# Recalibrating the build-time scheduler of a fused attention, expert and two-layer kernel: a floor on start times, measured durations, weight lows on VectorE, paced conversion

## The chip, the cores and the metric

The kernel runs on one core of one Trainium2 chip. The metric is the device time of one execution in microseconds (us); lower is better. The engines are TensorE (PE in the profile, with its weight loads as PEld), VectorE (DVE), ScalarE (ACT), GpSimd (POOL) and SyncE (SP), which here only issues DMAs. Each engine runs its own instructions in the order in which the program lists them, and waits on semaphores for the others.

## The reference

```python
attn = softmax(scale * q @ k.T, causal window of 64)      # 4 batches, 8 heads, 576 tokens, width 64
x    = (attn @ v).reshape(2304, 512)
e    = argmax(x @ w_gate + modality_bias[modality_id])    # one of 8 experts per token
x    = gate_w * (relu(x @ w1[e]) @ w2[e])                 # 512 -> 1024 -> 512
h    = x @ w_in                                           # 512 -> 2048
out  = (h - tanh(h)) @ w_out                              # 2048 -> 512
```

`w_in` and `w_out` come as float64, everything else as float32.

## The kernel before, in words

Full float32 precision is made of two reduced-precision parts: each operand is split into a high part and a low part (operand minus its high part), and each product is three matmuls, high by high, low by high, high by low. So every weight tile needs a **high copy** (`wh`, a cast) and a **low** (`wl`, a subtraction).

There are two stages. The **second stage** (`second`, the two-layer part) is a loop written out by hand; it starts on TensorE when the first stage's last matmul is done. The **first stage** (`front`) holds everything else:

- Attention runs in 36 groups (9 for each batch): scores (line 560), softmax on ScalarE, VectorE and GpSimd, transposes (line 584), values (line 605).
- Routing runs once for each batch (`route`): logits, softmax gate, expert ids, and a table of token positions. The gated rows go to memory as `xs`. After the last batch `unit_table` makes a table of the remaining work in some 55 tiny VectorE instructions (lines 818 to 966).
- The experts run as 5 units of tokens (units 0 to 3 have 504 tokens, unit 4 has 288). Units 0 and 1 can start while attention still runs. A unit gathers its rows with 4 GpSimd DMAs (`xg`, line 1033), transposes them on TensorE (line 1051) and splits them (`xh`, `xl`). Its **layer 1** is 96 matmuls (line 1125) with hidden parts `hh` on ScalarE (line 1156) and `hl` on VectorE (line 1159) in 8 pieces; its **layer 2** is 96 matmuls (line 1145) in 4 pieces. The 16 weight tiles of a unit are loaded to `raw`, and split by `t_wsplit` to `wh` and `wl`, in rings of 4 buffers each. `t_ids` turns a unit's token ids with one small TensorE transpose (line 1186) of `pif`, which VectorE copies (line 1183).
- The conversion (`t_conv`, 32 tiles) makes float32 bits out of the float64 words of `w_in` and `w_out`: two ScalarE instructions, three VectorE ones (lines 1220, 1222, 1224, here called the conversion's three steps) and a GpSimd addition (lines 1228 or 1235); 12 of the tiles are then split too (`winH`, `winL`, line 1241).

What sets the order of the first stage is a list scheduler that runs when the program is built. Each piece of work is a generator (a thread) that yields an `Op`: engine choices with a planned duration, tokens that it waits for, buffer rings, a PSUM bank, a priority. `Flow.pick` takes the op that can start first by the plan, lets ops with several engine choices go to the one that ends first (with `BIAS` added for VectorE), and writes the instruction; that fixes each engine's order. The chip does not follow the plan's times, only its order. An op with no engine (`Op(None, deps)`) is a group of conditions:

```python
            if not op.eng:
                return None, t, th
```

In the kernel before, the time at which such a group held is forgotten: the thread's next op, if it names no token itself, may be planned earlier than that time.

Of the kernel before, what the change touches and what calls it, by code (L numbers as in the profile page):

```python
# [109 lines left out]
class Flow:  # L110

    LAG = dict(PE=0.3, DVE=0.08, ACT=0.08, POOL=0.1, SP=0.0)
    BIAS = dict(DVE=0.3)
    LOOK = 0.05

    def __init__(self):
        self.free = dict(PE=6.0, DVE=5.0, ACT=5.0, POOL=8.0, SP=3.0)
        self.wire, self.th, self.n = 0.0, [], 0
        self.bank = [Tok(0.0) for _ in range(8)]

    def add(self, gen, prio):
        self.n += 1
        th = [prio, self.n, gen, None]
        self.th.append(th)
        self.step(th, None)

    def step(self, th, r):
        try:
            th[3] = th[2].send(r)
        except StopIteration:  # L130
            self.th.remove(th)

    def ready(self, op):
        t = 0.0
# [16 lines left out]
    def pick(self):  # L151
        best = {}
        for th in self.th:
            op = th[3]
            t = self.ready(op)
            if t is None:
                continue
            if not op.eng:
                return None, t, th
            e = min(op.eng, key=lambda e: max(self.free[e], t) + op.eng[e] + (len(op.eng) > 1) * self.BIAS.get(e, 0.0))  # L160
            best.setdefault(e, []).append((max(self.free[e], t), th))
        assert best, "nothing can go on"
        e = min(best, key=lambda e: min(s for s, _ in best[e]))
        lo = min(s for s, _ in best[e]) + self.LOOK
        prio = lambda th: (th[0] if th[3].prio is None else th[3].prio, th[1])
        s, th = min((x for x in best[e] if x[0] <= lo), key=lambda x: prio(x[1]))
        return e, s, th

    def run(self):
        while self.th:  # L170
            e, s, th = self.pick()
            op, r = th[3], Done()
            r.e, r.s, r.rel = e, s, [g.take() for g in op.rings]
            r.t = s
# [12 lines left out]


class Kernel:
# [179 lines left out]
    def t_load(self):  # L369
        nc, ap, at, R = self.nc, self.ap, self.at, self.rings  # L370

        def qk(pi):
            r = yield Op(("SP", DQ if pi == 0 else 2 * DQ), rings=[R["qk"]], prio=2.25 * pi - 4, wire=2.1)
            if pi:
                self.load_qk(pi)
            self.raw["qkr", pi] = r.rel[0]
            self.tk("qk", pi).t = r.t

        def tail(b):
            r = yield Op(("SP", 2 * DQ), rings=[R["tl"]], prio=9 * b, wire=1.1)  # L380
            tl = at.tile([128, 8, 64], F32, name="tl")
            nc.sync.dma_start(tl[64:128], ap["k"][b, :, 512:576, :].rearrange("h p d -> p h d"))
            nc.sync.dma_start(tl[0:64], ap["q"][b, :, 512:576, :].rearrange("h p d -> p h d"))
            self.raw["t", b] = tl, r.rel[0]
            self.tk("tl", b).t = r.t

        def v(pi):
            b, hp = divmod(pi, 4)
            h0 = 2 * hp
            r = yield Op(("SP", 2 * DQ), rings=[R["va"]], prio=2.25 * pi - 2, wire=1.1)  # L390
            va = at.tile([128, 4, 2, 64], F32, name="va", bufs=3)
            vb = at.tile([128, 3, 2, 64], F32, name="vb", bufs=3)
# [4 lines left out]
            r = yield Op(("SP", 2 * DQ), [r.tok], prio=2.25 * pi - 1, wire=0.5)
# [240 lines left out]
    def t_xrow(self, t):  # L638
# [13 lines left out]
        else:  # L652
            nc.vector.tensor_scalar(xr, pf, g, None, op0=ALU.mult)
        bk.t = r.t
        r = yield Op(("SP", DQ), [r.tok], wire=0.9)
        nc.sync.dma_start(self.xs[t * 128 : t * 128 + 128, :], xr)
        rel.t = r.t
        self.tk("xs", t).t = r.t
# [311 lines left out]
    def t_flag(self, okB, tok):  # L970
# [1 line left out]
        r = yield Op(("POOL", 1.4), [tok])  # L972
        self.Ti = self.cp.tile([BR, E * NSLOT], I32, name="Ti")
        nc.gpsimd.tensor_copy(self.Ti, self.T)
        r = yield Op(("PE", 0.1), [tok], bank=self.bankX)
        ps, bk = self.bt(r, 128, 1), r.bt
        nc.tensor.matmul(ps, self.ones[0:1, :], okB, start=True, stop=True)
        r = yield Op(("DVE", 0.6), [r.tok])
# [44 lines left out]
    def t_gather(self, i):  # L1023
# [2 lines left out]
        u = self.us[i]  # L1026
        yield Op(None, self.tks("xs", range(u.rows)))
        for j, _, _ in u.blocks:
            r = yield Op(("POOL", 1.12), [], [R["xg"]] if j == 0 else [], wire=0.9, lag=6.0)
            if j == 0:  # L1030
                u.xgr = r.rel[0]
                u.xg = mo.tile([BR, CB, DM], F32, name="xg")
# [57 lines left out]

    def t_wsplit(self, i, s, w, tok, rel):
        nc, mo, R = self.nc, self.mo, self.rings
        r = yield Op(dict(ACT=0.62, DVE=0.45), [tok], [R["wh"]])
        hi, rh = mo.tile([128, DM], F32R, name="wh", bufs=NW), r.rel[0]
        self.copy(r, hi, w)
        self.ws[i, s, 0] = hi, rh
        self.tk("ws", i, s, 0).t = r.t
        r = yield Op(dict(DVE=0.69, POOL=1.4), [r.tok], [R["wl"]])
        lo, rl = mo.tile([128, DM], F32R, name="wl", bufs=NW), r.rel[0]
        self.eng(r).tensor_tensor(lo, w, hi.bitcast(F32), op=ALU.subtract)  # L1100
        rel.t = r.t
# [74 lines left out]
    def t_ids(self, i):  # L1176
# [4 lines left out]
        rel = r.rel[0]  # L1181
        f = self.cp.tile([BR, CB], F32, name="pif")
        nc.vector.tensor_copy(f[:, :n], u.ids[:, :n])
        r = yield Op(("PE", 0.2), [r.tok], bank=self.bankX)
        ps, bk = self.bt(r, n, BR), r.bt
        nc.tensor.transpose(ps, f[:, :n], self.idF[:BR, :BR])
        r = yield Op(("DVE", 0.2), [r.tok])
# [12 lines left out]

    def t_conv(self, n, t):
        nc, cv, R = self.nc, self.cv, self.rings
        yield Op(None, [self.tk("w", *t), self.tk("O", CONV0)])
        r = yield Op(("SP", DQ), [], [R["craw"]], wire=1.8)
        raw, rr = self.conv_load(*t), r.rel[0]
        hi = raw.rearrange("p (n two) -> p n two", two=2)[:, :, 1]
        hf = raw.bitcast(F32).rearrange("p (n two) -> p n two", two=2)[:, :, 1]
# [520 lines left out]
```

## Time and profile before

| | |
|---|---|
| median of 3 runs | 812.12 us (810.32 to 814.28) |
| the profiled execution's own time | 808.94 us |
| its span, first to last instruction | 807.2 us |
| TensorE busy | 751.1 us (93%) |
| VectorE busy | 654.5 us (81%) |
| ScalarE busy | 504.3 us (62%) |
| GpSimd busy | 338.1 us (42%) |

The span is what the trace covers; the profiled execution's time is 1.7 us more. Busy shares are means over two stages that are limited differently: in the second stage TensorE is never idle for long, so the shares say little about the first. Times within the trace count from its first instruction.

### The profile page before, as it was taken

How to read it: one execution, taken by the hardware profiler on the slowest of the kernel's cores; microseconds unless marked ns; L12 is line 12 of the kernel's file. 1: busy time of each engine (PE TensorE's matmuls, PEld its weight loads, DVE VectorE, ACT ScalarE, POOL GpSimd, SP SyncE). 2: the span in 40 equal slices, each digit the busy share in tenths (PEclk: the TensorE clock that was granted, in tenths of full speed). 3: DMA queues.
4: the chain of work that ended last, by engine and by line, in shares of the span. 5: the costliest groups of instructions: out<-in, count | busy, mean ns of one | idle time of the engine just before them, and what ended most of it. 6: DMA issues, size and time to landing. Idle time of an engine off the chain costs nothing.

```text
span 807.2 us, 13452 instructions
## 1 busy us (share of the span) xinstructions
PE 751.1 (93%) x4489; PEld 655.1 (81%) x4495; DVE 654.5 (81%) x1140; ACT 504.3 (62%) x1195; POOL 338.1 (42%) x324
## 2 busy tenths in 40 slices
PE   6999859898969879999899999999999999999994
PEld 5888748677848667789888999988999989999893
DVE  4777829779999999827599888888888888888873
ACT  4788728663544454312789777777776767777662
POOL 3424235525656575220669344333324424434222
PEclk9999969999979989999999999999999999999997
DMA  9878767464768775535101011010101101001001
GB/s 192 161 184 191 195 139 213 130 220 148 232 213 255 234 206 169 160 117 159 36 1 40 0 40 30 11 40 10 31 1 40 40 0 40 22 1 39 1 2 43
DMA packets 131733, 80.39 MB, mean 100 GB/s; under 512 B 67988, under 2 KB 124820, under 8 KB 131654
## 3 DMA queue, kind: packets, MB, share of 16 engines
q1 hardware_dynamic: 127350, 69.55, 31.9%
q0 software_dynamic: 3264, 9.63, 3.9%
q8 instruction: 37, 0.61, 0.3%
q14 instruction: 42, 0.34, 0.2%
q10 hardware_dynamic: 1040, 0.26, 0.1%
HBM read 62.10 MB, written 14.16 MB: 94 GB/s over the span
## 4 chain that ended last, share of the span: by engine, by line
PE 75%; DVE 13%; issue 5%; POOL 2%; ACT 2%; DMA 2%; DVEq 0%; POOLq 0%; ACTq 0%
PE ps_g L1528 24%; PE ps_q L1574 24%; PE bank L1145 7%; PE bank L1125 6%; PE bank L560 4%; PE bank L605 2%; PE bank L584 2%; DVE hl L1159 1%; DVE wh L303 1%; DVE cva L1220 1%; POOL xg L1033 1%; DVE cva L1224 1%; DVE wl L1100 1%; DMA xg<-xs,ids 1%; PE bank L450 1%
## 5 line engine op out<-in xcount | busy, mean ns | idle before, releaser
L1559 POOL TENSOR_TENSOR gl<-gv,gh 128x384 fp32r<-128x384 f32 x94 | 100.5, 1070 | 167.5 <-ACT gh L1558 167.2
L1550 DVE COPY_PREDICATED gv<-gm,gt 128x384 f32<-128x384 int32 x96 | 110.8, 1154 | 9.9
L1574 PE MATMUL ps_q<-H,gh 128*128 128x512 f32 x288 | 113.5, 394 | 0.0
L1574 PE MATMUL ps_q<-H,gl 128*128 128x512 f32 x288 | 113.1, 395 | 0.2 <-DVE gl L1559 0.2
L1558 ACT ACTIVATE gh<-gv 128x384 fp32r<-128x384 f32 x96 | 50.3, 524 | 90.9 <-issue 77.4
L1546 DVE SCALAR_TENSOR_TENSOR gv<-gu,ps_g 128x384 f32<-128x384 f32 x96 | 52.9, 551 | 42.9 <-ACT gt L1543 42.3
L1548 DVE SCALAR_TENSOR_TENSOR gv<-gs,gv 128x384 f32<-128x384 f32 x96 | 77.3, 805 | 3.3
L1100 POOL TENSOR_TENSOR wl<-raw,wh 128x512 fp32r<-128x512 f32 x30 | 44.0, 1467 | 57.3 <-DVE wh L303 21.3
L1574 PEld LDWEIGHTS ps_q<-H,gl 128*128 128x128 f32 x288 | 54.0, 188 | 13.3 <-DVE gl L1559 0.7
L1547 DVE SCALAR_TENSOR_TENSOR gv<-gs,gv 128x384 f32<-128x384 f32 x96 | 60.1, 626 | 3.3
L580 POOL TENSOR_TENSOR P<-P,rc 128x512 f32<-128x512 f32 x36 | 38.0, 1058 | 58.8 <-DVE rc L578 26.9
L1542 ACT ACTIVATE gs<-gu,pa 128x384 f32<-128x384 f32 x96 | 58.0, 604 | 5.7 <-DVE gv L1548 5.7
L1541 ACT ACTIVATE gs<-gu,pa 128x384 f32<-128x384 f32 x96 | 59.3, 618 | 3.4 <-DVE gv L1547 0.2
L1574 PEld LDWEIGHTS ps_q<-H,gh 128*128 128x128 f32 x288 | 54.1, 188 | 8.9
L1545 ACT ACTIVATE gm<-gu,pth 128x384 f32<-128x384 f32 x96 | 58.0, 604 | 0.0
L574 ACT ACTIVATE P<-bank,nm 128x128 f32<-128x128 f32 x144 | 50.8, 373 | 7.7 <-DVE nm L571 7.5
L1549 DVE TENSOR_TENSOR gt<-ps_g,gt 128x384 f32<-128x384 f32 x96 | 52.7, 549 | 0.0
L303 DVE CAST wh<-raw 128x512 fp32r<-128x512 f32 x60 | 35.2, 591 | 19.1 <-PE bank L1145 17.2
L1100 DVE TENSOR_TENSOR wl<-raw,wh 128x512 fp32r<-128x512 f32 x50 | 43.9, 885 | 3.6 <-PE bank L1125 1.9
L1540 ACT ACTIVATE gu<-ps_g 128x384 f32<-128x384 f32 x96 | 45.4, 473 | 0.0
L1145 PE MATMUL bank<-hh,wh 128*128 128x504 f32 (+1 forms) x160 | 40.0, 385 | 5.5 <-ACT hh L1156 3.4
L1543 ACT ACTIVATE gt<-ps_g 128x384 f32<-128x384 f32 x96 | 45.0, 469 | 0.0
(420 smaller groups left out, 2105.3 us busy)
## 6 DMA issues: line engine op xcount, KB each, us to landing
raw<-in_w SPq DMA_DIRECT2D x80, 256.0 KB, 3.2
craw<-in_wout SPq DMA_DIRECT2D x16, 512.0 KB, 4.8
craw<-in_win SPq DMA_DIRECT2D x16, 512.0 KB, 4.7
xs<-xr SPq DMA_DIRECT2D x18, 256.0 KB, 2.2
kr<-in_k SPq DMA_DIRECT2D x16, 256.0 KB, 4.0
va<-in_v SPq DMA_DIRECT2D x32, 128.0 KB, 3.4
yd<-ys SPq DMA_DIRECT2D x16, 252.0 KB, 3.5
qr<-in_q SPq DMA_DIRECT2D x15, 256.0 KB, 4.3
```

Source lines behind the costliest of these rows:

```text
L1100: self.eng(r).tensor_tensor(lo, w, hi.bitcast(F32), op=ALU.subtract)
L1145: nc.tensor.matmul(ps, wt[:, k % 4, :], h, start=(q == 0), stop=(q == 3 * NF1 - 1))
L1528: nc.tensor.matmul(ps, w[:, c, :], x[:, c, :], start=(c == 0 and i == 0), stop=(c == 3 and i == 2))
L1541: nc.scalar.activation(s1, u, AF.Square, bias=self.pa1)
L1542: nc.scalar.activation(s2, u, AF.Square, bias=self.pa2)
L1545: nc.scalar.activation(m, u, AF.Relu, bias=self.pth)
L1546: nc.vector.scalar_tensor_tensor(v, u, cA, ps, op0=ALU.mult, op1=ALU.mult)
L1547: nc.vector.scalar_tensor_tensor(v, s1, b1, v, op0=ALU.add, op1=ALU.mult)
L1548: nc.vector.scalar_tensor_tensor(v, s2, b2, v, op0=ALU.add, op1=ALU.mult)
L1550: nc.vector.copy_predicated(v, m.bitcast(I32), t)
L1559: (nc.vector if last else nc.gpsimd).tensor_tensor(gl, v, gh.bitcast(F32), op=ALU.subtract)
L1574: nc.tensor.matmul(self.po[t], g[:, t * 128 : t * 128 + 128], w, start=(f == 0 and i == 0), stop=(f == NF2 - 1 and i == 2),)
```

## The change

It keeps, for each thread, the time at which a group of conditions held (`th[4]`, the floor) and plans no later op of that thread, or of a thread that it starts, before it. It replaces planned durations and DMA lags, raises the bias against VectorE for ops with a choice, lets weight lows (`wl`, `winL`) go to VectorE alone, has the conversion of tile n wait in the plan until 118 + 6.3 n, and plans the two small transposes of `t_ids` and `t_flag` 8 us after their inputs.

```diff
+CONVT, CONVP = 118.0, 6.3
+SLACK = 8.0
...
-    BIAS = dict(DVE=0.3)
+    BIAS = dict(DVE=0.6)
...
-        th = [prio, self.n, gen, None]
+        th = [prio, self.n, gen, None, self.floor]
...
     def step(self, th, r):
+        old, self.floor = self.floor, th[4]
         try:
             th[3] = th[2].send(r)
         except StopIteration:
             self.th.remove(th)
+        self.floor = old
...
             if t is None:
                 continue
+            t = max(t, th[4])
...
+            else:
+                th[4] = s
...
-        r = yield Op(("PE", 0.2), [r.tok], bank=self.bankX)
+        r = yield Op(("PE", 0.2), [Tok(r.t + SLACK)], bank=self.bankX)
...
-            r = yield Op(("POOL", 1.12), [], [R["xg"]] if j == 0 else [], wire=0.9, lag=6.0)
+            r = yield Op(("POOL", 1.12), [], [R["xg"]] if j == 0 else [], wire=0.9, lag=8.0)
...
-        r = yield Op(dict(ACT=0.62, DVE=0.45), [tok], [R["wh"]])
+        r = yield Op(dict(ACT=0.63, DVE=0.62), [tok], [R["wh"]])
...
-        r = yield Op(dict(DVE=0.69, POOL=1.4), [r.tok], [R["wl"]])
+        r = yield Op(dict(DVE=0.78), [r.tok], [R["wl"]])
...
-        yield Op(None, [self.tk("w", *t), self.tk("O", CONV0)])
-        r = yield Op(("SP", DQ), [], [R["craw"]], wire=1.8)
+        yield Op(None, [self.tk("w", *t), self.tk("O", CONV0), Tok(CONVT + CONVP * n)])
+        r = yield Op(("SP", DQ), [], [R["craw"]], wire=1.8, lag=4.0)
...
-        r = yield Op(dict(DVE=0.69, POOL=1.4), [r.tok])
+        r = yield Op(dict(DVE=0.78), [r.tok])
```

No instruction is added or removed but for those that change their engine. Counted over the first stage: the 80 weight lows stood on VectorE 50 times and on GpSimd 30 times, and now stand on VectorE 80 times; the 12 `winL` 8 and 4 times, now 12 and 0; the 80 high copies on VectorE 60 and on ScalarE 20 times, now 25 and 55. Fourteen small copies move from VectorE to ScalarE. The changed file has 6 lines more above line 200 or so and 7 below, so line 1051 there is 1058.

Three places where the order changes follow. The first is TensorE's order where unit 0's gathered rows (`xg`) are transposed; `kr` and `qr` are keys and queries of the next head pair, `P` and `PT` softmax results, `mG` and `mF` the mask. Before:

```order
L605 MATMUL bank_1754<-PT,va 64x64 x2
L455 MATMUL bank_1764<-idF,qr 128x128 x4
L1051 MATMUL bank_1779<-idF,xg 128x126 x4
L550 LDWEIGHTS idB
L550 MATMUL bank_1786<-mG,idB 128x512
L560 MATMUL bank_1786<-kT_88,qbd_85 128x128 x4
L450 MATMUL bank_1801<-idF,kr 128x128 x4
L455 MATMUL bank_1808<-idF,qr 128x128 x4
L1051 MATMUL bank_1816<-idF,xg 128x126 x4
```

With the change, TensorE again, at unit 0's transposes:

```order
L591 MATMUL bank_2177<-idF,P 128x128 x4
L822 LDWEIGHTS ones
L822 MATMUL bank_2183<-cc,ones 1x8
L557 LDWEIGHTS idB
L557 MATMUL bank_2189<-mG,idB 128x512
L567 MATMUL bank_2189<-kTt_91,qbt 128x128 x4
L1058 MATMUL bank_2210<-idF,xg 128x126 x4
L1058 MATMUL bank_2222<-idF,xg 128x126 x4
L1058 MATMUL bank_2230<-idF,xg 128x126 x4
L612 MATMUL bank_2246<-PT,va 64x64 x4
```

Before, the first of these transposes stood ahead of the last 8 of the 36 groups' scores and the last 11 groups' values; now all 36 scores and 31 groups' values stand ahead of it, the routing of the third batch with them.

The second is TensorE's order between layers 1 and 2 of unit 2, at the small transpose of `pif`. Before:

```order
L1125 MATMUL bank_3786<-xl,wh 128x504 x4
L1125 MATMUL bank_3786<-xh,wl 128x504 x4
L1186 MATMUL bank_3819<-idF,pif 4x126
L1145 MATMUL bank_3822<-hh_100,wh 128x504
L1145 MATMUL bank_3822<-hh_101,wh 128x504
L1051 MATMUL bank_3828<-idF,xg 128x126 x4
L1051 MATMUL bank_3840<-idF,xg 128x126 x4
```

With the change, the same transpose in layer 2 of unit 2:

```order
L1152 MATMUL bank_3823<-hh_106,wh 128x504
L1152 MATMUL bank_3823<-hh_107,wh 128x504
L1193 MATMUL bank_3845<-idF,pif 4x126
L1152 MATMUL bank_3823<-hh_100,wl 128x504
L1152 MATMUL bank_3823<-hh_101,wl 128x504
```

It stood ahead of layer 2's first matmul and now stands inside layer 2's second piece, behind 32 of its 96 matmuls.

The third is VectorE's order at the table of the remaining units (from `nB` on) and unit 0's last hidden low, `hl_115`. Before:

```order
L774 TENSOR_TENSOR ob<-ob,t_161 128x630
L1159 SCALAR_TENSOR_TENSOR hl_115<-bank_2612,hh_107 128x504
L789 TENSOR_REDUCE ccn<-oh 128x8
L790 TENSOR_TENSOR cc<-cc,ccn 128x8
L1100 TENSOR_TENSOR wl<-raw,wh 128x512
L793 TENSOR_TENSOR T<-T,bank_2704 126x160
L1183 CAST pif<-ids_1703 126x4
L1224 SCALAR_TENSOR_TENSOR cva<-craw,cva 128x512
L818 COPY nB<-bank_2729 1x8
L889 COPY cs_2749<-nB 1x1
```

With the change, VectorE where the table begins:

```order
L797 TENSOR_TENSOR cc<-cc,ccn 128x8
L1166 SCALAR_TENSOR_TENSOR hl_114<-bank_2624,hh_106 128x504
L800 TENSOR_TENSOR T<-T,bank_2653 126x160
L1227 TENSOR_SCALAR cva<-cva 128x512
L825 COPY nB<-bank_2680 1x8
L896 COPY cs_2692<-nB 1x1
```

And VectorE where it ends:

```order
L969 TENSOR_SCALAR fin<-dE,evl 1x1
L973 TENSOR_SCALAR okB<-over 1x1
L1166 SCALAR_TENSOR_TENSOR hl_115<-bank_2646,hh_107 128x504
L1071 TENSOR_TENSOR xl<-bank_2731,xh 128x504
L1071 TENSOR_TENSOR xl<-bank_2744,xh 128x504
L1107 TENSOR_TENSOR wl<-raw,wh 128x512 x2
```

Before, `hl_115` stood ahead of the table; now it stands behind all of it.

## Rows read from the trace of the kernel before

**Rows 1.** Busy time by stretches: stretch and length, each engine, granted clock, DMA.

```profile
50.00:100.00 50.00, 48.32 (x581) 43.25 (x585) 40.46 (x128) 40.86 (x156) 14.38 (x19) 1.00 0.76 189
211.00:324.00 113.00, 97.73 (x421) 78.28 (x420) 110.33 (x154) 52.50 (x92) 68.07 (x49) 0.92 0.71 211
```

**Rows 2.** Busy time by stretches again, where TensorE stood still.

```profile
100.00:116.00 16.00, 5.46 (x21) 4.44 (x22) 2.98 (x8) 1.98 (x9) 5.89 (x8) 0.59 0.82 181
188.00:192.00 4.00, 2.19 (x10) 1.47 (x8) 3.17 (x15) 1.11 (x3) 1.56 (x2) 1.00 0.65 190
225.00:240.00 15.00, 8.82 (x30) 6.01 (x28) 14.24 (x24) 6.70 (x12) 7.03 (x7) 0.66 0.66 209
279.00:292.00 13.00, 5.17 (x23) 3.96 (x22) 12.86 (x19) 6.41 (x12) 9.31 (x8) 0.74 0.65 187
```

**Rows 3.** Waits of TensorE up to 388 us: us in total, times, longest.

```profile
PE bank L1051 <- DMA xg<-xs,ids: 11.1, 4, 5.1
PE bank L1186 <- DVE pif L1183: 8.9, 2, 7.8
```

**Rows 4.** The chain that ended last: start us, us; routing logits of two batches.

```profile
46.78 1.11 PE bank L675 x16
...
75.97 1.11 PE bank L675 x16
```

**Rows 5.** VectorE's groups from 211 to 324 us: count, busy us, mean ns.

```profile
L1224 DVE SCALAR_TENSOR_TENSOR cva<-craw,cva 128x512 int32<-128x512 int32 x25 | 21.3, 853 | 0.4
L1100 DVE TENSOR_TENSOR wl<-raw,wh 128x512 fp32r<-128x512 f32 x19 | 20.8, 1107 | 0.2
L1222 DVE TENSOR_SCALAR cva<-cva 128x512 int32<-128x512 int32 x25 | 19.5, 778 | 0.6
L1220 DVE TENSOR_SCALAR cva<-cva 128x512 f32<-128x512 f32 x24 | 17.0, 708 | 0.0
L303 DVE CAST wh<-raw 128x512 fp32r<-128x512 f32 x25 | 17.0, 690 | 0.0
```

**Rows 6.** Tiles wl, wh and cva over the whole trace: ns min/median/max, first and last start.

```profile
L1100 DVE TENSOR_TENSOR wl<-raw,wh x50: 661/687/3491, 139.9 to 382.4; 128x512 fp32r<-128x512 f32 x50
...
L303 DVE CAST wh<-raw x60: 404/422/1525, 124.9 to 380.9; 128x512 fp32r<-128x512 f32 x60
...
L301 ACT ACTIVATE wh<-raw x20: 613/622/638, 126.9 to 381.8; 128x512 fp32r<-128x512 f32 x20
...
L1220 DVE TENSOR_SCALAR cva<-cva x32: 407/420/1524, 135.5 to 316.2; 128x512 f32<-128x512 f32 x32
L1222 DVE TENSOR_SCALAR cva<-cva x32: 405/428/1519, 136.4 to 316.7; 128x512 int32<-128x512 int32 x32
L1224 DVE SCALAR_TENSOR_TENSOR cva<-craw,cva x32: 671/693/2262, 137.5 to 317.1; 128x512 int32<-128x512 int32 x32
```

**Rows 7.** Timeline near 209 us, VectorE and then GpSimd: start us, us.

```profile
208.99 1.52 DVE L1220 TENSOR_SCALAR cva<-cva 128x512 f32<-128x512 f32 x1
...
208.93 1.30 POOL L1241 TENSOR_TENSOR win3L<-cvw,win3H 128x512 fp32r<-128x512 f32 x1 [0.74 <-ACT win3H L1239]
```

**Rows 8.** GpSimd's largest group from 211 to 324 us.

```profile
L1100 POOL TENSOR_TENSOR wl<-raw,wh 128x512 fp32r<-128x512 f32 x14 | 21.5, 1539 | 16.2 <-PE bank L1125 6.6 <-DVE wh L303 6.1 <-issue 2.6
```

**Rows 9.** Timeline of VectorE, the unit table's first and last instruction.

```profile
177.73 0.15 DVE L818 COPY nB<-bank 1x8 f32<-1x8 f32 x1
...
191.47 0.13 DVE L966 TENSOR_SCALAR okB<-over 1x1 bf16<-1x1 f32 x1
```

**Rows 10.** Timeline of TensorE at layer 2 of units 0 and 3: a wait stands in brackets.

```profile
181.79 1.99 PE L1145 MATMUL bank<-hh,wh 128*128 128x504 f32 x8
183.62 2.00 PE L1145 MATMUL bank<-hh,wl 128*128 128x504 f32 x8
...
337.73 0.27 PE L1186 MATMUL bank<-idF,pif 126*4 126x126 f32 x1 [1.10 <-DVE pif L1183]
```

**Rows 11.** Tile xr: GpSimd's part of what feeds the second stage's first chunk.

```profile
L1020 POOL TENSOR_TENSOR yl<-xr,yh x4: 1014/1109/1467, 321.9 to 333.1; 128x384 fp32r<-128x384 f32 x4
```

More of the change, by code (lines that the diff above doesn't have):

```diff
@@ L117, in __init__ @@
         self.free = dict(PE=6.0, DVE=5.0, ACT=5.0, POOL=8.0, SP=3.0)
-        self.wire, self.th, self.n = 0.0, [], 0
+        self.wire, self.th, self.n, self.floor = 0.0, [], 0, 0.0
         self.bank = [Tok(0.0) for _ in range(8)]
@@ L372, in qk @@
         def qk(pi):
-            r = yield Op(("SP", DQ if pi == 0 else 2 * DQ), rings=[R["qk"]], prio=2.25 * pi - 4, wire=2.1)
+            r = yield Op(("SP", DQ if pi == 0 else 2 * DQ), rings=[R["qk"]], prio=2.25 * pi - 4, wire=2.4)
             if pi:
@@ L379, in tail @@
         def tail(b):
-            r = yield Op(("SP", 2 * DQ), rings=[R["tl"]], prio=9 * b, wire=1.1)
+            r = yield Op(("SP", 2 * DQ), rings=[R["tl"]], prio=9 * b, wire=1.2)
             tl = at.tile([128, 8, 64], F32, name="tl")
@@ L389, in v @@
             h0 = 2 * hp
-            r = yield Op(("SP", 2 * DQ), rings=[R["va"]], prio=2.25 * pi - 2, wire=1.1)
+            r = yield Op(("SP", 2 * DQ), rings=[R["va"]], prio=2.25 * pi - 2, wire=1.2)
             va = at.tile([128, 4, 2, 64], F32, name="va", bufs=3)
@@ L396, in v @@
             self.tk("va", pi).t = r.t
[L397 removed]
+            r = yield Op(("SP", 2 * DQ), [r.tok], prio=2.25 * pi - 1, wire=0.8)
             nc.sync.dma_start(vb[0:64], va[64:128, 0:3])
@@ L654, in t_xrow @@
         bk.t = r.t
-        r = yield Op(("SP", DQ), [r.tok], wire=0.9)
+        r = yield Op(("SP", DQ), [r.tok], wire=1.0, lag=2.6)
         nc.sync.dma_start(self.xs[t * 128 : t * 128 + 128, :], xr)
@@ L974, in t_flag @@
         nc.gpsimd.tensor_copy(self.Ti, self.T)
-        r = yield Op(("PE", 0.1), [tok], bank=self.bankX)
+        r = yield Op(("PE", 0.1), [Tok(r.t + SLACK)], bank=self.bankX)
         ps, bk = self.bt(r, 128, 1), r.bt
@@ L1218, in t_conv @@
         tb = r.tok
-        yield Op(("DVE", 0.43), [ta])
+        yield Op(("DVE", 0.5), [ta])
         v.tensor_scalar(x, x, bits(0x38000000), bits(0x47EFFFFF), op0=ALU.max, op1=ALU.min)
-        yield Op(("DVE", 0.43))
+        yield Op(("DVE", 0.5))
         v.tensor_scalar(a, a, 0x07FFFFFF, 3, op0=ALU.bitwise_and, op1=ALU.logical_shift_left)
-        r = yield Op(("DVE", 0.69))
+        r = yield Op(("DVE", 0.78))
         v.scalar_tensor_tensor(a, hi, -0x40000000, a, op0=ALU.bitwise_and, op1=ALU.bitwise_or)
```

## The prediction

> **What bounds the kernel now.** I read the page first. TensorE is busy nearly all the time, and the second stage, from about 388 us, leaves it hardly a gap; the change doesn't touch its instructions. So I ask where TensorE stands still before 388 us, since each microsecond that it gains there moves the whole second stage. Next I read busy time by stretches. Early attention runs at TensorE's pace: 48.3 of 50 us [rows 1], and a batch of nine groups takes 29.2 us from one routing to the next, 3.2 us a group [rows 4]. From 211 to 324 us it is VectorE that never rests: 110.3 of 113 us, while TensorE has 97.7 and ScalarE 52.5 [rows 1].
>
> Smaller stretches then show four places where TensorE stands still [rows 2]. Idle time is length less busy time. After three of them the granted clock falls to its lower level, 1.2 of 2.4 GHz, for part of the stretch; what that costs I estimate as busy time times the missing share of the clock.
> - A, 100 to 116 us: 10.5 idle, 5.46 x 0.41 = 2.2 of clock: 12.8. TensorE's waits name the cause: unit 0's transposes wait 11.1 us for the gather `xg` [rows 3], and attention stands behind them.
> - T, 188 to 192 us: 1.8 idle, at the end of the unit table.
> - B, 225 to 240 us: 6.2 idle, 3.0 of clock: 9.2.
> - C, 279 to 292 us: 7.8 idle, 1.3 of clock: 9.2. Here the small transpose of `pif` waits for VectorE, 7.8 us at once [rows 3].
>
> Together 33.0 us. B and C lie in VectorE's saturated stretch: there VectorE sets the end, and TensorE waits for its lows.
>
> **Why VectorE is saturated.** Its groups in that stretch show means far above the same instruction's minimum: the three conversion steps take 708, 778 and 853 ns on average there, `wl` 1107, `wh` 690 [rows 5]; their minima are 407, 405, 671, 661 and 404 [rows 6]. The excess is 24 x 0.301 + 25 x 0.373 + 25 x 0.182 + 19 x 0.446 + 25 x 0.286 = 36.7 us of 113. The timeline shows where it comes from: a conversion step starts at 208.99, 0.06 us after a GpSimd subtraction, and takes 1.52 us instead of 0.42; it ends 0.28 us after GpSimd does [rows 7]. So a GpSimd instruction in SBUF holds up the VectorE one beside it.
>
> **The change, part by part.**
>
> *Lows to VectorE, high copies to ScalarE, conversion paced.* I count VectorE's rows in the order between unit 1's first hidden low and unit 3's first, which is this stretch: lows 18 before and 32 with the change, high copies 25 and 11, converted tiles 24 and 17, `winL` 6 and 4, two `ys` copies and none. At medians [rows 6] that is +14 x 0.687 - 14 x 0.422 - 7 x (0.420 + 0.428 + 0.693) - 2 x 0.69 - 2 x 0.69 (the last two priced as lows) = -9.8 us. The GpSimd lows that leave took 21.5 us [rows 8] of its 68.1 busy us there [rows 1]; if the excess falls by their share, 32%, that is 11.6 more. Bounds: nothing of the 36.7 comes back, or all. VectorE then needs 110.3 - 9.8 - 11.6 = 88.9 us (64 to 100.5) for what TensorE does in 97.7 - 4.3 (clock in B and C) = 93.4. I take 88.9: TensorE becomes the later one, by little, and B and C go (18.4). At 100.5 VectorE stays the bound, and the stretch still falls from 113 to 100.5. Fourteen more high copies cost ScalarE 14 x 0.622 = 8.7 us; it had 60 us free.
>
> A rule of the Trainium skill speaks against this part: Perfetto Trace Analysis, "Optimizing Scalar/DVE Operations", says that work may be offloaded from a saturated DVE to Scalar or even GPSIMD; the change takes lows the other way. The same paragraph warns that GPSIMD and DVE share an SBUF port, so offloading between these two might not help; the 1.52 us step agrees with the warning. By the first half alone the stretch would not fall by 9.8 but rise; that is a rival below.
>
> *Floor and longer DMA lag: unit 0's transposes move.* Before, they stood ahead of the last 8 groups' scores; now all 36 scores and 31 of 36 groups' values stand ahead of them. At 3.2 us a group that is some 20 us of TensorE work put in front of a wait of 11.1. GpSimd issues the gather three softmax groups later than before (28 instead of 25), which is up to 10 us; 20 still covers it, just. I take all of A, 12.8; bound below 5, if the gather lands late.
>
> *The small transposes.* The `pif` transpose stands 32 matmuls deeper, 7.4 us at 0.23 each (8 in 1.84 us [rows 10]), so it no longer is what waits; without VectorE's relief this alone would only hand C's wait to the hidden lows. It counts for nothing by itself, and T is already in the list.
>
> *What gets worse.* First, the order puts unit 0's last hidden low behind the whole unit table on VectorE. The table took 13.9 us before, from 177.7 to 191.6 [rows 9], and one low 0.69. TensorE's order from the table's counts to the matmul that needs that low holds 6 matmuls of layer 1, 23 of layer 2 (0.23 each, 6.7 us), and 12 short transposes that I count as nothing. So TensorE waits up to 7.9 us; less if the table runs quicker with GpSimd quiet. Queued behind it are unit 1's `xl` and the lows of layer 2. I take 4 and 2 for the slower clock afterwards: +6 (2 to 10). Second, a boundary between layers 1 and 2 cost 1.1 us even at unit 3, where VectorE was not behind [rows 10]; B and C hid this at units 1 and 2, and unit 3's stays: I take three such boundaries, +3.3 (0 to 8). Third, the conversion now ends in unit 4's layer 1, so the second stage's first chunk is split behind the last matmuls: the last GpSimd part, 1.1 us [rows 11], stands behind unit 4's last copy. TensorE needs it only for the last quarter of its first twelve matmuls: +1 (0 to 4, if its load lands late).
>
> Sum: -12.8 - 1.8 - 18.4 + 6 + 3.3 + 1 = **-22.7 us**. The profiled execution took 808.94 us, so 786.2. The median shown is 812.12, 3.2 us above it; I set the same saving against that: 812.1 - 22.7 = 789.4, **789 us**.
>
> **The rivals.**
> - *VectorE keeps the pace.* No excess comes back (100.5 us) and the new waits are at their upper bounds: -12.8 - 1.8 - 12.5 + 10 + 8 + 4 = -5.1: 807 us. For it: 88.9 against 93.4 is a thin margin, and 30 of the 32 GpSimd additions of the conversion now stand behind the table. Against it: GpSimd loses 21.5 us of lows there.
> - *The lows only load a saturated engine* (the rule's first half). 34 lows come to VectorE, 34 x 0.687 = 23.4; 35 copies leave, 35 x 0.422 = 14.8; +8.6 on VectorE's path, B and C stay. A and T go: 812.1 - 12.8 - 1.8 + 8.6 + 6 + 1 = 813 us, no change. Against it stands the count: in this stretch seven conversions leave too.
> - *The relay of weights* (slower). A high copy on ScalarE followed by a low on VectorE is 0.622 + 0.687 = 1.31 us with a handoff, and ScalarE has hidden copies `hh` that wait for TensorE in the same queue. If none of the 35 moved pairs is hidden: 35 x 1.31 = 45.8, and 812.1 - 22.7 + 45.8 = 835 us. It turns the sign when more than 17 of the 35 are unhidden. Against it: rings of four tiles, 12 matmuls a tile in layer 1, so three tiles are 8 us of cover.
> - *No new waits*: the 33.0 come back whole, 779 us.
>
> **How the numbers follow.** Chances: the forecast (781 to 797) 0.58; VectorE keeps the pace (797 to 808) 0.20; no new waits (776 to 781) 0.05; the lows only load (808 to 816) 0.08; slower by the relay or a wait like it 0.09. Within 0.5%, about 4 us, a measurement of this kernel can't be told from no change. So faster 0.83, same 0.08, slower 0.09. The range from 776 to 806 leaves out the last two cases and the upper edge of the second, about 0.2; its low end is 33.0 back and 3 more of smaller waits.
>
> **What would show it.** In the trace with the change: no wait of unit 0's transposes over 3 us and no fall of the clock near 100 us; between unit 1's and unit 3's first hidden low about 97 us instead of 113, with TensorE the busiest engine; VectorE's conversion steps near their medians; a new wait of TensorE for `hl` after the unit table; the second stage starting some 23 us earlier and then taking as long as before. The prediction is wrong if VectorE is still above 97% busy in that stretch, if TensorE waits for `wh` or `wl` at tile after tile, or if the gather still holds TensorE.

## The result, and the profile after

The changed kernel takes 773.5 us (median of 4 runs, 772.2 to 774.14) beside 811.22 us for the kernel before on the same chip: ratio 0.9527, 95% interval 0.9496 to 0.9559. It is faster, as forecast, by 15.9 us more than the forecast of 789.4, and outside the range of 776 to 806. The profiled executions took 808.94 and 774.14 us, 34.8 less.

The page of the changed kernel: span, busy time by engine, and the granted clock in 40 slices.

```profile
span 772.3 us, 13418 instructions
PE 741.8 (96%) x4495; PEld 651.5 (84%) x4495; DVE 631.7 (82%) x1125; ACT 526.7 (68%) x1244; POOL 286.2 (37%) x290
PEclk9999999999999999999999999999999999999998
```

The clock row has no dip left. Busy time by stretches of the changed kernel (stretch and length, each engine, granted clock, DMA), the counterparts of [rows 1, 2]: where the gather was waited for; after the unit table; unit 1's first hidden low to unit 3's first (211 to 324 us before).

```profile
100.00:116.00 16.00, 15.05 (x189) 13.29 (x188) 11.50 (x34) 13.82 (x58) 10.25 (x12) 1.00 1.12 249
165.00:172.00 7.00, 5.05 (x27) 3.92 (x26) 5.88 (x21) 2.85 (x6) 1.11 (x1) 1.00 0.56 189
190.00:282.00 92.00, 92.00 (x421) 75.73 (x420) 81.95 (x130) 52.56 (x94) 31.78 (x25) 1.00 0.77 232
```

In the third row TensorE is busy for all 92.00 us, and VectorE, with 81.95, has 10 us to spare. TensorE's waits up to 388 us, answering [rows 3]:

```profile
PE bank L457 <- DMA kr<-in_k: 6.0, 1, 6.0
PE ps_g L1535 <- DVE gt L1556: 3.7, 2, 2.3
PE bank L1152 <- DVE hl L1166: 2.0, 1, 2.0
PE bank L612 <- ACT PT L308: 1.8, 3, 0.7
PE bank L591 <- POOL P L587: 1.6, 2, 0.9
...
PE ps_g L1535 <- POOL yl L1027: 0.6, 1, 0.6
PE ps_g L1535 <- ACT yh L1025: 0.2, 1, 0.2
```

The gather `xg` and `pif` are gone from the list. The first line is the start, as before; `ps_g` belongs to the second stage. The largest new wait in the first stage is for `hl`, 2.0 us; short ones in attention and routing, for `PT`, `oh` and `kT`, are new too. VectorE's groups from 190 to 282 us, answering [rows 5], and then GpSimd's largest there:

```profile
L1107 DVE TENSOR_TENSOR wl<-raw,wh 128x512 fp32r<-128x512 f32 x32 | 31.7, 1006 | 1.7 <-ACT wh L308 1.5
L1231 DVE SCALAR_TENSOR_TENSOR cva<-craw,cva 128x512 int32<-128x512 int32 x18 | 14.0, 779 | 0.5
L1166 DVE SCALAR_TENSOR_TENSOR hl<-bank,hh 128x504 fp32r<-128x504 f32 x17 | 11.6, 682 | 4.5 <-ACT hh L1163 4.4
L1227 DVE TENSOR_SCALAR cva<-cva 128x512 f32<-128x512 f32 x18 | 8.6, 479 | 1.0 <-ACT cva L1221 1.0
L1229 DVE TENSOR_SCALAR cva<-cva 128x512 int32<-128x512 int32 x18 | 7.7, 425 | 0.5
L310 DVE CAST wh<-raw 128x512 fp32r<-128x512 f32 x11 | 5.3, 482 | 1.1 <-PE bank L1152 1.0
...
L1040 POOL DMA_INDIRECT xg<-xs,ids x7 | 7.4, 1052 | 9.9 <-DVE cva L1231 5.4 <-PE bank L1058 3.0 <-issue 1.5
```

Two of the three conversion steps are near the medians of [rows 6] and the third, 779 ns, not far above its 693; `wl` still takes 1006 ns on average against a median of 687, but no wait for it stands in the list.

Where the time came from, counted on both traces from TensorE's first matmul of one part to its first of the next (us):

| part | before | after | measured | forecast |
|---|---|---|---|---|
| start to layer 2 of unit 0 (A) | 174.0 | 160.4 | -13.6 | -12.8 |
| layer 2 of unit 0 (T, and the hidden low) | 27.9 | 26.4 | -1.5 | -1.8 + 6 |
| units 1 to 3 (B, C, the boundaries) | 160.3 | 138.1 | -22.2 | -18.4 + 3.3 |
| unit 4 | 25.6 | 25.6 | 0 | 0 |
| second stage | 419.5 | 422.0 | +2.5 | +1 |

### The profile page after: what moved, and what is told of

Same layout as the page of the kernel before. It is cut to its first block, busy times and chain, and to the rows that moved or that the text cites. A ratio compares the mean times of both kernels' runs of the same rounds, so it can differ in the third digit from the quotient of the medians.

```text
span 772.3 us, 13418 instructions
## 1 busy us (share of the span) xinstructions
PE 741.8 (96%) x4495; PEld 651.5 (84%) x4495; DVE 631.7 (82%) x1125; ACT 526.7 (68%) x1244; POOL 286.2 (37%) x290
## 4 chain that ended last, share of the span: by engine, by line
PE 90%; DVE 3%; issue 2%; ACT 1%; DMA 1%; POOL 1%; SPq 0%; DVEq 0%; POOLq 0%; ACTq 0%
PE ps_g L1535 25%; PE ps_q L1581 25%; PE bank L1132 13%; PE bank L1152 12%; PE bank L567 4%; PE bank L612 3%; PE bank L591 2%; PE bank L1058 1%; PE bank L557 1%; PE bank L457 1%; PE bank L462 1%; DMA kr<-in_k 1%; PE bank L651 1%; PE bank L682 1%; PE bank L699 0%
## 5 line engine op out<-in xcount | busy, mean ns | idle before, releaser
L1557 DVE COPY_PREDICATED gv<-gm,gt 128x384 f32<-128x384 int32 x96 | 110.9, 1156 | 10.3 <-ACT gu L1547 0.5
L1107 DVE TENSOR_TENSOR wl<-raw,wh 128x512 fp32r<-128x512 f32 x80 | 72.5, 919 | 4.3 <-ACT wh L308 3.3
L1163 ACT ACTIVATE hh<-bank 128x504 fp32r<-128x504 f32 (+1 forms) x40 | 22.3, 558 | 35.4 <-PE bank L1132 35.2
L308 ACT ACTIVATE ys<-bank 128x504 f32<-128x504 f32 (+1 forms) x20 | 11.1, 556 | 44.2 <-PE bank L1152 28.8
L1132 PE MATMUL bank<-xh,wh 128*128 128x504 f32 (+1 forms) x160 | 41.1, 376 | 0.0
```

Of the source, the lines that this page charges most:

```text
L1132: nc.tensor.matmul(ps, wt[:, k, :], xt[:, k, :n], start=(k == 0 and q == 0), stop=(k == 3 and q == 2))
L1557: nc.vector.copy_predicated(v, m.bitcast(I32), t)
```

## The experiments

Each profiled run is split in the same parts (unit 4, left out, takes 25.5 to 25.7 us, in e15 27.7); the medians of the kernel before were 810.93 (e1 to e4), 809.52 (e5 to e8), 809.14 (e9 to e12) and 810.09 us (e13 to e16).

| kernel | to layer 2 of unit 0 | layer 2 of unit 0 | units 1 to 3 | second stage | median us | ratio, interval |
|---|---|---|---|---|---|---|
| e1 before, lows on VectorE | 175.9 | 26.0 | 156.1 | 420.1 | 805.27 | 0.9929, 0.9898 to 0.9960 |
| e3 before, floor | 164.9 | 31.9 | 161.2 | 419.4 | 804.64 | 0.9933, 0.9894 to 0.9972 |
| e7 before, high copies | 177.3 | 33.8 | 152.1 | 419.4 | 810.57 | 1.0014, 0.9993 to 1.0036 |
| e10 before, prices, lags, slack | 179.7 | 25.5 | 153.8 | 419.8 | 807.91 | 0.9988, 0.9972 to 1.0003 |
| e15 before, floor and pacing | 168.8 | 28.5 | 147.4 | 420.9 | 795.03 | 0.9822, 0.9788 to 0.9856 |
| e9 before, high copies, lows | 175.6 | 29.9 | 146.3 | 420.0 | 799.09 | 0.9867, 0.9827 to 0.9907 |
| e14 the same with conversion prices | 183.8 | 28.4 | 138.6 | 418.6 | 796.70 | 0.9834, 0.9808 to 0.9860 |
| e2 after, 30 lows on GpSimd | 163.9 | 27.1 | 138.1 | 420.8 | 776.66 | 0.9583, 0.9540 to 0.9627 |
| e4 after, no floor | 179.9 | 25.4 | 138.1 | 419.7 | 791.82 | 0.9770, 0.9713 to 0.9828 |
| e5 after, old high copies | 167.1 | 26.3 | 138.0 | 419.4 | 777.29 | 0.9585, 0.9520 to 0.9651 |
| e6 after, no pacing | 165.2 | 26.4 | 138.1 | 419.5 | 777.43 | 0.9587, 0.9523 to 0.9650 |
| e8 after, no slack | 162.0 | 26.4 | 138.0 | 424.3 | 778.62 | 0.9601, 0.9540 to 0.9663 |
| e11 after, lows planned on both | 160.1 | 29.4 | 140.5 | 420.5 | 777.99 | 0.9615, 0.9581 to 0.9650 |
| e12 after, early lows, pace 5.3 | 160.3 | 28.4 | 137.9 | 420.0 | 772.35 | 0.9539, 0.9512 to 0.9565 |
| e13 after, additions at the table | 164.6 | 33.0 | 138.1 | 420.3 | 781.51 | 0.9639, 0.9612 to 0.9665 |
| e16 after, pace 5.3 | 162.8 | 27.9 | 138.3 | 418.6 | 775.17 | 0.9566, 0.9545 to 0.9587 |

**Which engine takes the lows (e1, e2).** The order stays the planner's; only the engine that runs a low changes. e1 is the kernel before with all of them on VectorE, e2 the changed one with 30 of 80 on GpSimd.

```diff
e1: -        self.eng(r).tensor_tensor(lo, w, hi.bitcast(F32), op=ALU.subtract)
    +        nc.vector.tensor_tensor(lo, w, hi.bitcast(F32), op=ALU.subtract)
    (the same for self.wL[t])
e2: -        self.eng(r).tensor_tensor(lo, w, hi.bitcast(F32), op=ALU.subtract)
    +        (nc.gpsimd if s % 8 in (2, 4, 7) else nc.vector).tensor_tensor(lo, w, hi.bitcast(F32), op=ALU.subtract)
```

> The order of before, planned as before; only the 30 weight lows and 4 winL that stood on GpSimd are written to VectorE at the same point of the program. Theory V (GpSimd holds VectorE up beside it, and that made the saturated stretch): VectorE gets 34 x 0.687 = 23 us more of its own work and is given back the excess that those 50 us of GpSimd caused; the two about cancel: 800 to 812 us, conversion steps near 0.42 us on average, wait A for the gather unchanged at 11 us. Rival L (lows only load a saturated engine): 811 + 15 to 23 = 826 to 834 us. Rival O (the order is what counts, engines do not): 811 us within 4, with the waits B and C as before.

> The order of the changed kernel, planned as it is; 30 of the 80 weight lows (three of each eight tiles) are written to GpSimd at the same point of the program. Theory V: VectorE has some 4 us of slack in 46 in each unit, is held up again, and TensorE waits for lows and hl: 780 to 795 us. Rival O (the order alone made the gain): 772 to 776 us.

e1 gains 5.7 us, where theory L had it lose 15 or more. VectorE stays the bound, 107.57 us busy of 111 (210 to 321 us). That is less than the 110.33 us of before, although it now runs the 14 `wl` there that GpSimd had. In e2 the window from 195 to 287 us, with three of VectorE's groups and GpSimd's largest:

```profile
195.00:287.00 92.00, 92.00 (x422) 75.63 (x421) 86.28 (x119) 51.76 (x93) 49.42 (x38) 1.00 0.75 233
...
L1107 DVE TENSOR_TENSOR wl<-raw,wh 128x512 fp32r<-128x512 f32 x21 | 27.1, 1300 | 4.5 <-ACT wh L308 4.3
L1227 DVE TENSOR_SCALAR cva<-cva 128x512 f32<-128x512 f32 x18 | 13.7, 762 | 0.6 <-ACT cva L1221 0.6
L1166 DVE SCALAR_TENSOR_TENSOR hl<-bank,hh 128x504 fp32r<-128x504 f32 x17 | 11.4, 674 | 0.7 <-ACT hh L1163 0.7
...
L1107 POOL TENSOR_TENSOR wl<-raw,wh 128x512 fp32r<-128x512 f32 x13 | 19.6, 1511 | 3.3 <-ACT wh L308 1.7 <-DVE wh L310 1.1 <-issue 0.4
```

VectorE runs 11 lows fewer than in the changed kernel, 7.5 us at 0.685, and is busy 4.3 us longer (86.28 against 81.95), because those that stay take 1300 ns and the first conversion step 762. So a low given to GpSimd saves VectorE nothing here. TensorE has no gap all the same, and theory V's 780 us or more was missed (776.66): there was cover to spare.

**The floor alone, and the change without it (e3, e4).**

```diff
e3, in the kernel before:      e4, in the changed kernel:
...
+            t = max(t, th[4])     -            t = max(t, th[4])
...
+            else:
+                th[4] = s
```

e3 also has the lines of the change that keep the floor for each thread.

> Before plus the floor alone (old durations, lows on either engine, no slack, no pacing). Theory V: wait A for the gather (11.1 us and its slow clock, 12.8 together) goes, waits B and C of VectorE's saturated stretch stay: 811 - 13 = 798 us, 794 to 802. Rival O: the floor alone brings nearly the whole gain, below 782 us.

> The changed kernel without the floor (and so without any effect of the pacing, whose token stands in a group of conditions). Theory V: unit 0's transposes stand 8 groups earlier again and wait for the gather: 773.5 + 13 = 786 us, plus up to 10 for a conversion that crowds VectorE early: 784 to 797. Rival O: back to 805 us or more.

TensorE's waits in e3, and the first of e4:

```profile
PE bank L1056 <- DVE xl L1069: 7.2, 2, 4.2
PE bank L1150 <- DVE hl L1164: 6.0, 1, 6.0
...
PE bank L1057 <- DMA xg<-xs,ids: 10.7, 3, 6.2
```

With the floor the gather's wait is gone; without it, it is back with 10.7 us, the part up to layer 2 of unit 0 takes 19.5 us longer, and the kernel 18.3 by medians (791.82 against 773.5). Not all of that is the floor's: the pacing needs the floor, since without it the time that a group of conditions held is forgotten, so e4 loses both. Against e6, which lacks the pacing alone, the floor is worth 14.7 us in that part and 14.4 by medians. In the kernel before, the floor gained 9.1 us there and gave back 4.0 behind the table, where TensorE now waits 6.0 us for `hl`; the time falls by 6.3, less than the 9 or more that theory V had.

**Other parts one by one (e5 to e8, e11).**

```diff
e5, in the changed kernel:  BIAS = dict(DVE=0.3), dict(ACT=0.62, DVE=0.45) for wh
e6, in the changed kernel:  CONVT, CONVP = 0.0, 0.0
e7, in the kernel before:   BIAS = dict(DVE=0.6), dict(ACT=0.63, DVE=0.62) for wh
e8, in the changed kernel:  SLACK = 0.0
e11, in the changed kernel: dict(DVE=0.78, POOL=1.4) for wl and wL
```

> The changed kernel with the old bias (0.3) and old high-copy durations: 45 of the 80 high copies stand on VectorE instead of 25, conversions paced as in the change. Theory H (taking high copies off VectorE is what ended its saturation): 20 more copies at 0.45 to 0.7 us put VectorE back near 100% of units 1 and 2: 780 to 790 us. Theory P (spreading the conversion is what ended it): 773 to 777 us, TensorE unbroken through units 1 to 3.

> The changed kernel without pacing (tokens at 0): 25 of 32 conversions are done by unit 2's layer 2 instead of 20 to 24, 18 high copies on VectorE. Theory P: waits for hl and hh come back at units 1 and 2: 780 to 795 us. Theory H: high copies are still on ScalarE, so units 1 to 3 stay unbroken: 772 to 777 us.

> Before plus only the new bias and high-copy durations: 30 high copies on VectorE instead of 60, 58 lows on VectorE and 22 on GpSimd, conversions as early as before. Theory H: VectorE loses 30 x 0.6 = 18 us before unit 3, gains 8 lows; waits B and C shrink by half or more: 795 to 803 us, wait A stays. Theory P: within 4 of 811 us, since the conversion still crowds units 1 and 2.

> The changed kernel with the slack of the small transposes set to 0. My theory: with VectorE no longer behind, the transposes wait at most 1 us each at five boundaries: 773.5 to 778 us. Rival (the slack is what removed wait C, 9 us, and the 1.1 us at unit 3): 780 us or more.

> The changed kernel with one part undone: the planner may put lows on GpSimd again at 1.4 us (it puts 33 of 80 there). Theory (several parts, each spare): units 1 to 3 stay unbroken at 22.0 and 23.8 to 24.5 us a layer; the lows that stay on VectorE and its conversion steps get longer beside GpSimd's; 775 to 779 us. Rival (lows on VectorE alone are what gave B and C back): TensorE stands more than 4 us in unit 1 or 2, 785 us or more.

Taken out of the changed kernel, each costs 3 to 5 us by medians (one and the same stretch of program differs by 4.1 us between two profiles, last section), and units 1 to 3 stay at 138.0 or 138.1, but in e11, 140.5. So theory H fails in e5 and theory P in e6: each forecast 780 us or more without its part. The rivals of e8 and e11 fail too. e7 shows a gain given back, and H's 795 to 803 us missed: units 1 to 3 fall by 8.2 us, but the last hidden low comes behind the table with GpSimd busy, TensorE waits 7.0 us for `hl`, and the time is the old one.

**Combinations on the kernel before (e9, e10, e14, e15).**

```diff
e9:  e7's two lines, and dict(DVE=0.69) for wl and wL
e14: e7's two lines, dict(DVE=0.78) for wl and wL, and the conversion's three steps at 0.50, 0.50, 0.78
e10: the changed kernel without e4's line, with e5's and e11's
e15: e3's lines, and Tok(118.0 + 6.3 * n) among the conversion's conditions
```

> The kernel before with two parts of the change: the new durations of high copies (and the bias), and lows planned on VectorE alone. No floor, no pacing, old durations of the conversion and of the transfers, the small transposes without slack. Theory (several parts, each spare): these two together are enough to let VectorE fall behind TensorE's pace in units 1 and 2; the four layer lengths of units 1 and 2 read 22.0, 23.8 to 24.5, 22.0, 23.8 to 25, the stretch from unit 1's first hidden low to unit 3's first takes 91 to 95 us, the gather wait stays, and the time is 788 to 795 us. Rival (the new durations of the conversion, the lags and the slack of the small transposes carry B and C): the small transposes still wait for VectorE by more than 4 us in unit 1 or 2, the stretch takes over 100 us, 800 to 810 us.

> The kernel before with only the new durations of the conversion and of the transfers, the longer lags, and the slack of the small transposes: no floor, old high copies, lows allowed on GpSimd. Theory (several parts, each spare): not enough alone; the stretch from unit 1's first hidden low to unit 3's first stays over 100 us with VectorE over 95% busy, and the time is 800 to 808 us. Rival (these durations carry B and C): units 1 and 2 unbroken at 22.0 and 23.8 to 24.5 us a layer, the stretch 91 to 95 us, 788 to 795 us.

> The kernel before with the new high copies, the lows on VectorE at the new price, and the new prices of the conversion's steps (0.50, 0.50 and 0.78 us): no floor, no pacing, no longer lags, no slack. Theory (what counts is how many conversions stand in units 1 and 2; by the order 23 do here, 24 in the kernel before, 19 to 21 in those where TensorE has no gap): not quite enough; units 1 to 3 take 141 to 146 us, 790 to 799 us. Rival (the planner's prices do it, the number of conversions does not matter): units 1 to 3 take 138 us, about 790 us or less.

> The kernel before with the floor and the pacing of the conversion (which does nothing without the floor), and all else as before: lows on both engines, old high copies and prices. Theory (fewer conversions in units 1 and 2 is worth as much as the other parts): units 1 to 3 take 145 to 155 us instead of 161 with the floor alone, and the time is 787 to 798 us. Rival (pacing is only worth something once lows and high copies have moved): 158 to 161 us, 801 to 806 us.

Unit 1's to unit 3's first hidden low in e9, e14 and e15:

```profile
210.00:313.00 103.00, 98.04 (x434) 80.05 (x433) 96.07 (x145) 64.31 (x115) 40.40 (x32) 0.97 0.76 233
...
217.00:311.00 94.00, 93.78 (x427) 76.72 (x426) 88.86 (x138) 63.75 (x114) 38.65 (x30) 1.00 0.86 258
...
203.00:300.00 97.00, 94.44 (x423) 77.00 (x422) 85.62 (x129) 40.75 (x71) 47.61 (x35) 0.98 0.66 206
```

e9's forecast was missed: high copies and lows alone leave VectorE 96.07 of 103 us busy and 8.2 us of the 22.2 unrecovered. With the conversion's prices beside them (e14) TensorE has hardly a gap any more (0.2 us), although 22 conversions stand in the stretch: the number of conversions there, which I had taken for the measure, doesn't decide it. Its time is 796.70 us only because layer 2 of unit 0 starts at 183.8, after waits of 8.6 us for the gather, 6.3 for `P` and 5.5 for `qbd` (queries laid out for the scores). e10 answers as the theory had it, 102.7 us from hidden low to hidden low, and no gain in time. In e15 only 16 conversions stand in the stretch, and TensorE still waits there, 2.6 us for `xl`, and 4.5 behind it, at units 3 and 4, for `pif`, which has no slack in this run.

**Work put beside the table (e13).**

```diff
+        nc.vector.tensor_copy(self.ltT[0:1, 0:8], n)
+        for _ in range(5):
+            nc.gpsimd.tensor_tensor(self.ltT[:, 0:512], self.ltT[:, 0:512], self.ltT[:, 0:512], op=ALU.add)
         s = cum(n, "cs")
```

> The changed kernel, with five GpSimd additions of 128x512 in an old tile put beside VectorE's unit table (and one copy of eight numbers on VectorE that starts them). Nothing else reads what they write. Theory (the wait for unit 0's last hidden low came out small because GpSimd is quiet beside the table): the table takes 13 to 14 us instead of 9.4, some of its short instructions over 0.8 us, and the wait for the hidden low grows from 2.0 to between 5 and 7 us; 777 to 780 us. Rival (the table is short for another reason, such as where it stands): the table stays below 10.5 us and the wait below 3 us, 773 to 775 us.

TensorE's wait in e13, then GpSimd's additions, two instructions of the table, and TensorE's stretches behind it:

```profile
PE bank L1155 <- DVE hl L1169: 5.9, 1, 5.9
...
163.26 5.51 POOL L904 TENSOR_TENSOR ltT<-ltT 128x512 f32<-128x512 f32 x5 [14.57 <-DVE ltT L902]
...
164.42 1.02 DVE L896 COPY cs<-cs 1x4 f32<-1x4 f32 x1
165.53 1.02 DVE L907 TENSOR_TENSOR st<-cs,nB 1x8 f32<-1x8 f32 x1
...
173.00:180.00 7.00, 3.18 (x12) 2.81 (x13) 5.02 (x21) 1.70 (x3) 0.00 (x0) 0.71 0.52 190
180.00:188.00 8.00, 8.00 (x31) 6.56 (x31) 7.60 (x11) 3.83 (x8) 5.92 (x6) 0.83 0.86 238
```

In the changed kernel the same place reads (table's first and last instruction, the hidden low, and TensorE's matmul that needs it):

```profile
158.59 0.15 DVE L825 COPY nB<-bank 1x8 f32<-1x8 f32 x1 [0.33 <-PE bank L822]
159.29 0.16 DVE L896 COPY cs<-cs 1x4 f32<-1x4 f32 x1
167.84 0.13 DVE L973 TENSOR_SCALAR okB<-over 1x1 bf16<-1x1 f32 x1
167.90 0.66 DVE L1166 SCALAR_TENSOR_TENSOR hl<-bank,hh 128x504 fp32r<-128x504 f32 x1
...
168.61 0.50 PE L1152 MATMUL bank<-hl,wh 128*128 128x504 f32 x1 [1.95 <-DVE hl L1166]
```

The table takes 9.4 us alone and 13.3 beside five additions, much as in the kernel before (13.9, [rows 9]); five of its instructions, on a handful of numbers, then take 0.8 to 1.0 us instead of 0.15. The wait grows from 1.95 to 5.9 us, the clock falls after it (3.18 x 0.29 + 8.00 x 0.17 = 2.3 us), and layer 2 of unit 0 takes 6.6 us longer. The kernel takes 8.0 us longer by medians, somewhat more than either theory had; between the two profiles, 4.2 us of difference lie ahead of layer 2 of unit 0, and the second stage gives 1.7 back.

**Two tries at something better (e12, e16).**

```diff
e12 and e16: CONVT, CONVP = 118.0, 5.3
e12: +  prio=-11 if i == 0 else None   (on the hidden lows)
```

> A version meant to be better: the changed kernel with unit 0's hidden lows ahead of the unit table on VectorE (a priority), and the conversion paced at 5.3 us a tile instead of 6.3. Theory: the 2.0 us wait for the last hidden low of unit 0 goes, and the second stage's first chunk is split while unit 4's layers still run, so that the rest after the first stage takes 419.5 to 420.5 us instead of 422.0: 769 to 772 us. Rival: the table then ends later and the transposes or the loads behind it take the wait, and the faster conversion makes VectorE late again in unit 1: 774 us or more.

> The changed kernel with the conversion paced at 5.3 us a tile instead of 6.3, and nothing else. Theory: units 1 to 3 stay unbroken, the second stage starts without its ramp, so that the rest after the first stage is 420.0 us instead of 422.0: 770 to 772 us. Rival: what the second stage's start gains comes back as a wait in units 0 to 3: 773 to 775 us.

The second stage then takes 420.0 and 418.6 us, in neither is there a wait for `yl`, and TensorE's first twelve matmuls there take 2.1 us, as before, instead of 3.5: that much came from the late end of the conversion. It isn't the whole 2.5 us: in e5 the conversion ends as late, and the second stage takes 419.4. Yet in e12 the 2.0 us of `hl` became 2.4 us of `xl`, which now stands behind a longer table, and e16 loses 2.4 us to layer 2 of unit 0 (2.0 of them ahead of unit 0, where its program is still the changed kernel's) and 1.5 in it. There TensorE waits for `hl` just as long as in the changed kernel, 1.95 us, but then its clock falls. The stretch behind that wait, in the changed kernel and then in e16:

```profile
172.00:180.00 8.00, 8.00 (x37) 6.33 (x36) 7.32 (x10) 3.74 (x7) 6.98 (x5) 1.00 0.98 272
...
172.00:180.00 8.00, 8.00 (x35) 6.74 (x34) 6.78 (x13) 3.99 (x9) 4.72 (x5) 0.83 0.73 202
```

Of e16's 1.5 us, 8.00 x 0.17 = 1.4 are this clock. Neither time can be told from the changed kernel's: the intervals overlap. Both theories' times were missed, e12's by 0.35 us; of e12's rival the new wait came true, and e16's rival came near by its time, though no wait in units 0 to 3 grew.

## Why the prediction fell short

- **A, T, B, C (right in size, a little small; B's wait was misread).** The 33.0 us came back whole. The floor carries A: -13.6 measured, and 14 to 15 when taken out alone (e4 against e6). Units 1 and 2 gained 10.2 and 9.3 us for the 18.4 forecast. But "TensorE waits for its lows" holds for neither: C waits for `pif` [rows 3], and B for `hh`. The kernel before, ScalarE and then TensorE in B:

```profile
231.12 0.66 ACT L1214 ACTIVATE cva<-craw 128x512 f32<-128x512 f32 x1 [2.15 <-POOL wout7W L1228]
231.68 0.66 ACT L1217 ACTIVATE cvr<-craw 128x512 int32<-128x512 uint32 x1
232.24 0.57 ACT L1156 ACTIVATE hh<-bank 128x504 fp32r<-128x504 f32 x1
...
232.87 0.79 PE L1145 MATMUL bank<-hh,wh 128*128 128x504 f32 x1 [3.10 <-ACT hh L1156]
```

The hidden part `hh` stands in ScalarE's order behind two instructions of the conversion, and these wait for a GpSimd addition of an earlier tile (`cva` has two buffers), which waited 2.56 us for VectorE's conversion steps. In this way TensorE lost 5.5 of B's 6.2 us. VectorE still stands at the end of the chain, so relieving it helps; fewer conversions help too: in e9 and e15 there is no such wait from unit 1 to unit 3.
- **VectorE needs less time than TensorE (right, with a wider margin).** Forecast 88.9 us of VectorE's work against 93.4 of TensorE's, found 81.95 against 92.00. The excess over the minima was mis-sized: it did not fall by GpSimd's share of lows, 11.6 of 36.7 us; over the same minima [rows 6] 15.5 are left (32 x 0.345 for `wl`, 11.0, and 4.5 in the rest), so 21.2 came back. The term counted only the lows that leave GpSimd (21.5 us, [rows 8]); in the stretch it is busy 31.78 us instead of 68.1 [rows 1], since 7 of its 25 conversion additions and 2 `winL` leave too.
- **What gets worse (the step that failed).** +10.3 us were priced. The hidden low behind the table was to cost 4 and 2 of clock; it cost 2.0, and the clock stayed at 1.00. Of the wait's upper bound, 7.9, the table took 4.5 back (9.4 us instead of 13.9) and TensorE's work ahead of the wait 1.4 (8.1 us instead of 6.7, 1.1 of it the transposes counted as nothing). The place was right, and with GpSimd at work beside the table (e13) the price is there, even higher, 5.9 and 2.3; I had noted "less if the table runs quicker with GpSimd quiet" and then not taken it, though the same change empties GpSimd. That the clock cost nothing was partly luck: behind the same wait e16 lost 1.4 us by it. The three boundaries, +3.3, were none: the 1.1 us at unit 3 [rows 10] I had read as the boundary's own price, since VectorE seemed not behind there. It was VectorE's: unit 3 falls from 49.1 to 46.4 us, and in e8, where `pif` has no slack, TensorE has no wait from 190 to 352 us.
- **The second stage's start**: +1 forecast, +2.5 measured; 1.4 are the late conversion (e12, e16), the rest is open.
- **The base.** The forecast set its saving against the median of 812.12, the profiled execution lay 3.2 below it. The median after lies 0.6 below its own profiled execution. Of the 15.9 us, 12.1 are the terms and 3.8 this. Of the 12.1, 5.7 lie in layer 2 of unit 0, 7.1 in units 1 to 3 (3.3 the boundaries, 2.7 that unit 3 got shorter, 1.1 in units 1 and 2) and 0.8 in A; the second stage takes 1.5 back.
- **The rivals.** "No new waits" (779) came nearest, with a chance of 0.05. "VectorE keeps the pace" fell with VectorE's 81.95 us. "The lows only load" fell with e1, and VectorE's stretch shrank by 28 us. The advice that it rests on, and the warning beside it in the Trainium skill (Perfetto Trace Analysis, "Optimizing Scalar/DVE Operations"), are settled for these lows by e2: the warning holds here. The relay of weights never showed: no wait for `wl` or `wh` stands in the list.

**What carries units 1 to 3** is no single part. Put on the kernel before, the lows' engine gains 4.2 us there, high copies 8.2, the prices with lags and slack 6.5, the floor alone loses 0.9, floor and pacing gain 12.9, high copies with lows 14.0, and these with the conversion's prices 21.7, next to the 22.2 of all. Taken out singly, none costs over 2.4. By these sums, each part takes some of VectorE's load away until TensorE is the later one, and what goes beyond that is spare. The mean load alone doesn't tell when that is: TensorE has hardly a gap in e14 with VectorE 88.86 of 94 us busy, and waits in e15 with 85.62 of 97, so where an instruction stands in the order counts too. Open is how the 6.5 us divide among prices, lags and slack, which weren't tried apart.

## What to carry to other kernels

When a change empties an engine that holds up another, price the new waits in the state after it, not by the durations of before: a 13.9 us chain of tiny instructions was 9.4 long once its neighbour was quiet. When a saturated engine is relieved, look for the point where the next one takes over; parts beyond it measure little when removed singly, so test them on the old kernel too, and in pairs. A short wait on a saturated engine's result is no evidence of a price that stays when the saturation goes. And follow a wait to its end before you name its cause: the engine that releases it may itself stand behind other work.

## What the runs showed of the hardware

A GpSimd addition of 128x512 can hold up even a tiny VectorE instruction: one on a 1x4 tile took 1.02 us beside it and 0.16 alone. Not every kind is held: `hl`, which reads one operand from PSUM and one from SBUF, kept 674 ns in e2, where `wl`, with both in SBUF, took 1300. The Trainium skill (SBUF — State Buffer, "Who interferes with whom") says that a VectorE instruction with at most one SBUF input, outside its two-port modes, doesn't contend with GpSimd, that one with two does when GpSimd reads SBUF, and that copies can enter those modes; the two rows and the held copy agree, and no run here shows which mode that copy ran in.

Also, one program can pass one place with the clock up or down. Up to the table e13's program is the changed kernel's. From 114 to 120 us, the changed kernel and then e13:

```profile
114.00:120.00 6.00, 5.05 (x64) 4.50 (x63) 5.59 (x23) 4.62 (x15) 1.57 (x3) 1.00 1.14 221
...
114.00:120.00 6.00, 4.19 (x43) 3.92 (x41) 5.42 (x24) 3.65 (x15) 2.47 (x4) 0.82 0.97 211
```

There TensorE is idle 0.86 us longer in e13 and its clock falls; unit 0 starts 4.1 us later. Single profiles of near-equal kernels differ by that much before any edit acts, so parts are compared here, and medians for the whole. Whether the medians carry some of it too isn't shown.
